# Attention and gated MLP on one core: the row sums of the first 256 queries by matmul, an opening ordered anew

## The chip, the cores and the metric

The kernel runs on one core of a Trainium2 chip. A core has five engines that work beside one another, each with its own queue of instructions that it takes strictly in order: TensorE (PE; its weight loads are listed as PEld), VectorE (DVE), ScalarE (ACT), GpSimd (POOL) and SyncE (SP), which here issues the DMAs. An engine waits for another on semaphores. The metric is the device time in microseconds, from one launch.

## The reference

Eight batches of windowed attention over 8 heads, then a gated MLP on the result:

```python
# q, k, v: (8, 8, 576, 64)
scores = q @ k.T / 8 + slope_h * -(i - j);  masked to 0 <= i - j < 128
attn = exp(scores - max);  attn = attn / (sum(attn) + 1e-9)
x = (attn @ v) as (8, 576, 512)
h = relu(x @ w_in);  u, g = h[:, :, :512], h[:, :, 512:]
g = layer_norm(g);   g = einsum('ts,bsd->btd', w_spatial, g) + b_spatial
out = (u * g) @ w_out
```

w_in and w_out arrive as 64-bit words. They are turned into float32 on the chip, by four or five passes of DVE and ACT over each 128x512 piece (`bits64`).

## The kernel before, in words

Batches 1 to 7 run in a steady pattern: pairs of heads (28 pairs), each with its products (L794), a softmax (L808 to L848), a DMA transpose (L854) and the products with the values (L899), and then, for a whole batch, the units of the MLP: v (L983), u (L1046), s (the spatial product, L1067) and o (L1107).

Batch 0 is different, since nothing is loaded and no weight is converted yet. It works on tiles of 128 queries, named `t` (products, minimum and exponent: `raw_tile`) and `n` (transpose on PE, product with the values: `raw_out`), each digit pair being tile and head pair: `t02` is tile 0 of pair 2. In `raw_tile` PE writes the scores of two blocks into two of four PSUM banks `s`, DVE adds the table and takes the row's extreme (L705), and ACT takes the exponent and, with `accum_out`, the row sum (L709; the accumulator is then read by an instruction of its own). A step `m` (`raw_sums`, L717 and L718) waits for the row sums of all four pairs of a tile and takes the reciprocals. `raw_out` multiplies the probabilities by them (L730 on ACT or L731 on DVE), transposes (L738), copies (L412), multiplies with the values (L753) and copies the result out (L412) to `xt`. The MLP units of batch 0 are the same in float32: v at L976, u at L1038, o at L1099. The first u unit needs all four converted pieces of the u half of w_in; the last pass over such a piece is L449.

What sets the order: the kernel records its steps as a plan, each with an engine (or a choice between ACT and DVE), a weight in ns, a due time and the parts of buffers it reads and writes. A list scheduler (`forward`, `backward`) runs through the plan twelve times and writes the instructions in the order of the best pass. The string OPENING sets the order of recording of the first steps. The weights and due times decide what stands where in each queue; on the chip the queues are then fixed. On PE, 64 matmuls of a tile of ones with itself (`WARM`, L395) are steps of the plan too, and stand wherever the planner saw PE free. A last step adds further matmuls of that kind where the plan has an idle gap on PE (`filler`).

Of the kernel before, what the change touches and what calls it, by code (L numbers as in the profile page):

```python
# [9 lines left out]
F32 = mybir.dt.float32  # L10
# [5 lines left out]
AF = mybir.ActivationFunctionType  # L16
# [39 lines left out]
class Plan:  # L56
# [3 lines left out]

    PASSES, COLD, SLOW = 12, 6000, 9000
    LAG = {"PE": 200, "DVE": 130, "ACT": 130, "POOL": 150, "SP": 2200}

    def __init__(self):
# [42 lines left out]
    def forward(self, due):  # L109

        left = [len(x) for x in self.first]
        at, begun, ended, way = ([0] * len(left) for _ in range(4))
        ready = {e: [] for e in self.LAG}
        free = {**dict.fromkeys(self.LAG, 0), "SP": 700}
        events = [(0, n) for n, k in enumerate(left) if k == 0] + [(700, -1)]
        heapq.heapify(events)
        out, queued, now, dma, lanes = [], dict.fromkeys(self.LAG, 0), 0, 800, []
        while events or any(ready.values()):
            while events and events[0][0] <= now:
                n = heapq.heappop(events)[1]  # L120
                if n >= 0:
                    ways = self.ops[n][0]
                    ends = [max(free[w[0]], now) + queued[w[0]] + w[1] + (700 if w[0] == "DVE" and len(ways) > 1 else 0) for w in ways]
                    k = way[n] = ends.index(min(ends))
                    queued[ways[k][0]] += ways[k][1]
                    heapq.heappush(ready[ways[k][0]], (due[n], n, k))
            for e, heap in ready.items():
                if heap and free[e] <= now:
                    _, n, k = heapq.heappop(heap)
                    weight = self.ops[n][0][k][1]  # L130
                    queued[e] -= weight
                    if e == "SP":
                        dma = max(dma, now)
                        ended[n] = dma = dma + weight * (1.9 if dma < self.SLOW else 1)
                        lanes = [*lanes[-7:], dma + self.LAG[e]]
                        free[e] = max(now + (650 if now < self.SLOW else 500), lanes[0] if len(lanes) == 8 else 0)
                    else:
                        ended[n] = free[e] = now + weight * (2 if e == "PE" and now < self.COLD else 1)
                    begun[n] = now
                    end = ended[n] + self.LAG[e] + self.late.get(n, 0)  # L140
                    out.append(n)
                    heapq.heappush(events, (free[e], -1))
                    for a, whole in self.after[n]:
                        left[a] -= 1
                        at[a] = max(at[a], end if whole else now)
                        if left[a] == 0:
                            heapq.heappush(events, (at[a], a))
            if events:
                now = max(now, events[0][0])
        assert len(out) == len(self.ops)  # L150
        return max(ended), out, way, ended, begun
# [40 lines left out]
                self.filler(int((idle - self.SPARE) * self.FILL / self.filler_ns))  # L192
            self.ops[n][0][best[2][n]][2]()

    SPARE, FILL, UNTIL = 400, 0.5, 95000

    def idle(self, out, way, ended, begun):

        last = None
        for n in out:  # L200
            gap = 0
            if self.ops[n][0][way[n]][0] == "PE":
                if last is not None and self.SLOW < begun[n] < self.UNTIL and begun[n] - ended[last] > self.SPARE:
# [6 lines left out]
def attn_gmlp_kernel(ctx, tc, qk, v, w_in, w_spT, b_sp, w_out, outT):  # L210
# [3 lines left out]
    nc = tc.nc  # L214
# [14 lines left out]
    NB = S // D  # L229

    SWITCH = 190
    SCORES, VALUES, BOTH = 1600, 1800, 2760


    WX = 12
    OPENING = (
# [37 lines left out]
    def act(n, pointers=0):  # L274
        return (45, 188, 284)[pointers] + n / 1.18
# [4 lines left out]
    def pe(*cols):  # L280
        return sum(12 + n / 2.38 for n in cols)
# [1 line left out]
    def pe16(*cols):  # L283
        return sum(2.5 + n / 2.4 for n in cols)

    def dma(n):
        return n / 385


    nhalf = fixed([P, 1], F32, "nhalf")  # L290
# [34 lines left out]
    def xcols(x, a, c0, c1):  # L325
        return parts(x, c0, c1, 32, (a,))
# [220 lines left out]
    def wsp_load(c, due):  # L547
        st = raw_w[c] = plan.buf(work, f"wraw{c}", 1, [P, S], F32)

        def f():  # L550
            nc.sync.dma_start(st(), w_spT[c * P:(c + 1) * P, :])
        plan.add("SP", dma(P * S * 4), due - 4000, f, (), [(st, 0)])

        def f():
            nc.scalar.activation(wsp()[:, c, 1, :].bitcast(BF16), st(), AF.Abs)
        plan.add("ACT", act(S), due, f, [(st, 0)], [(wsp, (c, 1))])
# [75 lines left out]
    def load(b, p, due, pieces, raw=None):  # L632


        raw = raw or plan.buf(work, "qkraw", 3, [P, 2, S], F32)
        src = qk[b, 2 * p:2 * p + 2].rearrange("h d a s -> (h d) a s")
        for t0, t1, d in zip([0] + pieces, pieces, due):
            cs = slice(t0 * P, min(S, t1 * P))
            plan.add("SP", dma(P * 2 * (cs.stop - cs.start) * 4), d, lambda cs=cs: nc.sync.dma_start(raw()[:, :, cs], src[:, :, cs]),
                     (), [(raw, t) for t in range(t0, t1)])  # L640
        return raw

# [2 lines left out]
    def values_load(b, p, due):  # L645
        if b == 0 and p == NP - 1:
            vr = vr3
        else:
            vr = plan.buf(work, *(("vraw", NP) if b % 2 or b == 0 else (f"wraw{p}", 1)), [P, NQ, P], F32)
        vraw[b, p] = vr  # L650
        for t0, t1 in ((0, 2), (2, NQ)) if b == 0 else ((0, NQ),):
            plan.add("SP", dma(P * (t1 - t0) * P * 4), due + 15000 * (t0 > 0), lambda t0=t0, t1=t1: nc.sync.dma_start(vr()[:, t0:t1], v[b, p][:, t0:t1]),
                     (), [(vr, t) for t in range(t0, t1)])

    def values_limit(b, p, due):
# [27 lines left out]
    def raw_tile(p, t, k, raw, due):  # L683
# [15 lines left out]
        for e, i in enumerate(blocks):  # L699
            n = min(i + 1, 3) * D  # L700
            pr = lambda e=e, n=n: slot_ap(k)[:, W - n:W] if e == 0 else slot_ap(k)[:, 512 - n:]
            cols = slot_parts(k, e)

            def f(e=e, n=n, pr=pr):
                nc.vector.tensor_tensor_reduce(pr(), flat(e)[:, :n], tabs()[:, 2 * p + e, W - n:], -0.125, 3e38, ALU.add, ALU.min, st(NM_, e))  # L705
            plan.add("DVE", dve(n), due + 300, f, [(sc[e], 0), (tabs, 2 * p + e)], cols + [key(NM_, e)])

            def f(e=e, pr=pr):
                nc.scalar.activation(pr(), pr(), AF.Exp, bias=st(NM_, e), scale=-1.0, accum_out=st(SM_, e))  # L709
            plan.add("ACT", act(n, 2), due + 600, f, cols + [key(NM_, e)], cols + [key(SM_, e)])  # L710
# [10 lines left out]
    def raw_out(p, t, k, vr, xt, due):  # L721
# [2 lines left out]
        tiles = [x for x in (t - 1, t) if x >= 0]  # L724
        st = lambda e: rstat()[:, t % 2, RC_, e * NP + p:e * NP + p + 1]
        cols = [x for e in range(len(blocks)) for x in slot_parts(k, e)]
        for e, i in enumerate(blocks):
            n = min(i + 1, 3) * D
            pr = lambda e=e, n=n: slot_ap(k)[:, W - n:W] if e == 0 else slot_ap(k)[:, 512 - n:]
            plan.either([("ACT", act(n, 1), lambda e=e, pr=pr: nc.scalar.activation(pr(), pr(), AF.Copy, scale=st(e))),  # L730
# [15 lines left out]
        def f():  # L746
            for j in range(2):
                for n, x in enumerate(tiles):
                    c = n * P + j * D
                    ap = pf(c, c + D)  # L750
                    if len(blocks) == 2:
                        ap = bass.AP(ap.tensor, ap.offset, [ap.ap[0], [len(tiles) * P + D - 2 * j * D, 2], [1, D]])
                    nc.tensor.matmul(xp()[j * D:(j + 1) * D, :m], vr()[:, x, j * D:(j + 1) * D], ap,  # L753
                                     start=(n == 0), stop=(n == len(tiles) - 1), skip_group_check=True)
        plan.add("PE", SWITCH // 2 + 40 + pe(*[4 * m] * len(tiles)), due + 800, f, pcols + [(vr, x) for x in tiles], [(xp, 0)])
        qs = slice(t * P, t * P + m)
        copy(m, lambda: (xt()[:, qs], xp()[:, :m]), due + 1000, [(xp, 0)], xcols(xt, 0, qs.start, qs.stop))

    def clear():
# [380 lines left out]
    def record(kind, b, p):  # L1140
# [124 lines left out]
```

## Time and profile before

| | before |
|---|---|
| time, median of 3 runs | 535.12 us (535.08 to 535.28) |
| profiled execution, its own time | 535.35 us |
| its span, first to last instruction | 533.6 us |
| PE busy | 524.9 us, 98% |
| DVE busy | 441.4 us, 83% |
| ACT busy | 410.3 us, 77% |
| granted TensorE clock, mean | 1.000 |

The profiled execution lies 0.23 us above the median. Its span is 1.75 us shorter than its time. A busy share is an average over the whole span; the stages differ, and the rows below show them one by one. In the rows "128x192" is partitions by elements of one instruction; `idle before` is the time for which the engine did nothing ahead of it. DVE and ACT instructions overlap at their ends by some 0.1 us, so that what one costs its queue is the distance from its start to the next start, not its duration.

### The profile page before, as it was taken

The page shows a single profiled execution, that of the slowest core. Times are in us where ns is not written, and L with a number is a line of the kernel's source. Part 1 is how long each engine was busy: PE and PEld are TensorE (multiplying, and loading weights), DVE is VectorE, ACT ScalarE, POOL GpSimd, SP SyncE. Part 2 cuts the span into 40 slices and gives each one's busy share as a digit, 9 for nine tenths or more (in the row PEclk, how much of TensorE's full clock was granted, in tenths as well). Part 3 has the DMA queues.
Part 4 walks back from the last instruction along what each step waited for, and adds up shares of the span by engine and source line. Part 5 has one row for each costly group of instructions (what it writes and reads, how often), then busy time and mean ns, then how long its engine had stood idle before and what let it go on. Part 6 is the DMA issues. An engine that isn't in the chain of part 4 may idle for free.

```text
span 533.6 us, 15995 instructions
## 1 busy us (share of the span) xinstructions
PE 524.9 (98%) x6118; PEld 380.0 (71%) x6120; DVE 441.4 (83%) x1645; ACT 410.3 (77%) x1289; POOL 29.2 (5%) x75
## 2 busy tenths in 40 slices
PE   9999999999999999999999999999999999999997
PEld 5656567776687668885788758886688758784775
DVE  7999999999997787989999899888998898635440
ACT  7999999979986676969889778777977777634322
POOL 0000020001100010001100010000100010001000
PEclk9999999999999999999999999999999999999999
DMA  7987563987585433699768865765175435410002
GB/s 240 356 304 265 157 113 63 234 182 164 119 173 128 130 74 86 160 213 173 140 143 195 173 140 98 174 157 128 45 142 144 110 68 71 92 47 22 2 1 90
DMA packets 127809, 73.56 MB, mean 138 GB/s; under 512 B 105970, under 2 KB 118386, under 8 KB 127732
## 3 DMA queue, kind: packets, MB, share of 16 engines
q1 hardware_dynamic: 127732, 72.54, 57.7%
q8 instruction: 48, 0.79, 0.6%
q14 instruction: 29, 0.24, 0.1%
HBM read 37.13 MB, written 9.44 MB: 87 GB/s over the span
## 4 chain that ended last, share of the span: by engine, by line
PE 51%; DVE 3%; ACT 1%; issue 0%; DVEq 0%
PE m L1067 13%; PE m L1107 11%; PE m L1046 11%; PE m L983 8%; PE s L794 3%; PE x L899 3%; PE m L1012 1%; DVE pq L848 1%; DVE st L941 0%; DVE prob L808 0%; ACT pq L843 0%; DVE vt L954 0%; DVE vn L994 0%; PE s L899 0%; ACT prob L814 0%; DVE st L946 0%
## 5 line engine op out<-in xcount | busy, mean ns | idle before, releaser
L1067 PE MATMUL m<-wsp,vn 128*128 128x288 f16 x768 | 110.9, 286 | 0.0
L814 ACT ACTIVATE prob<-prob,stat 128x192 f32<-128x192 f32 (+2 forms) x252 | 107.0, 432 | 3.1 <-DVE stat L808 2.8
L843 ACT ACTIVATE pq<-prob,stat 128x192 f16<-128x192 f32 (+2 forms) x252 | 90.2, 429 | 3.9 <-DVE pq L848 1.3
L1067 PEld LDWEIGHTS <-vn 128*128 128x128 f16 x768 | 74.8, 98 | 19.6 <-issue 0.2
L1046 PE MATMUL m<-xt,win 128*128 128x288 f16 x672 | 88.1, 286 | 0.4 <-ACT vt L416 0.4
L848 DVE SCALAR_TENSOR_TENSOR pq<-prob,stat,pq 128x192 f16<-128x192 f32 (+2 forms) x252 | 86.9, 389 | 1.0 <-ACT pq L843 0.8
L1107 PE MATMUL m<-gs,wout 128*128 128x288 f16 x636 | 81.3, 286 | 0.0
L1046 PEld LDWEIGHTS <-win 128*128 128x128 f16 x672 | 65.1, 98 | 19.4 <-issue 1.5
L1107 PEld LDWEIGHTS <-wout 128*128 128x128 f16 x672 | 64.9, 98 | 16.5
L983 PE MATMUL m<-win,xt 128*128 128x512 f16 x336 | 75.5, 379 | 0.2 <-ACT o L1120 0.2
L808 DVE CUSTOM_DVE_ANT_0 prob<-s,tabs 128x192 f32<-128x192 f32 (+2 forms) x252 | 70.3, 329 | 5.9 <-PE s L794 5.7
L983 PEld LDWEIGHTS <-xt 128*128 128x128 f16 x336 | 32.2, 98 | 38.6 <-issue 2.4
L814 ACT ACTIVATION_READ_ACCUMULATOR prob<-prob,stat 128x1 f32 x252 | 49.3, 196 | 0.0
L1083 ACT ACTIVATE gs<-u 128x288 f16<-128x288 f32 x46 | 20.3, 441 | 37.6 <-DVE u L1080 37.2
L794 PE MATMUL s<-qkraw 64*64 64x192 f32 (+1 forms) x1008 | 43.4, 310 | 0.0
L1080 DVE SCALAR_TENSOR_TENSOR u<-m,u 128x288 f32<-128x288 f32 x56 | 25.5, 456 | 21.4 <-PE m L1067 20.5
L899 PEld LDWEIGHTS <-vh 64*64 64x64 f16 x1232 | 34.7, 106 | 9.5 <-issue 8.0
L899 PE MATMUL x<-pt,vh 64*64 64x192 f16 (+2 forms) x1188 | 38.3, 224 | 1.1 <-POOL am L910 1.1
L794 PEld LDWEIGHTS s<-qkraw 64*64 64x64 f32 x1008 | 36.3, 133 | 1.9 <-issue 1.6
L941 DVE BATCH_NORM_STATS2 st<-vt 128x6 f32<-128x512 f32 (+1 forms) x40 | 27.5, 688 | 12.2 <-ACT vt L416 11.8
L950 POOL TENSOR_TENSOR st<-st,nhalf 128x1 f32<-128x1 f32 (+1 forms) x40 | 25.4, 635 | 210.9 <-DVE st L946 179.8
L1087 DVE SCALAR_TENSOR_TENSOR gs<-gs,u 128x288 f16<-128x288 f16 x53 | 24.1, 455 | 10.1 <-ACT gs L1083 9.5
(187 smaller groups left out, 792.1 us busy)
## 6 DMA issues: line engine op xcount, KB each, us to landing
qkraw<-in_qk_dram SPq DMA_DIRECT2D x28, 576.0 KB, 5.0
out_dram<-o SPq DMA_DIRECT2D x63, 144.0 KB, 1.8
vraw<-in_v_dram SPq DMA_DIRECT2D x16, 320.0 KB, 3.7
wraw<-in_v_dram SPq DMA_DIRECT2D x12, 320.0 KB, 3.1
vn<-in_w_in_dram SPq DMA_DIRECT2D x4, 512.0 KB, 7.6
wout<-in_w_in_dram SPq DMA_DIRECT2D x4, 512.0 KB, 7.8
wout<-in_w_out_dram SPq DMA_DIRECT2D x4, 512.0 KB, 4.9
wraw<-in_w_spT_dram SPq DMA_DIRECT2D x4, 288.0 KB, 5.1
```

Source lines behind the costliest of these rows:

```text
L794: nc.tensor.matmul(flat(bank)[rows, c0:c0 + n], raw()[j * D:(j + 1) * D, 0, i * D:(i + 1) * D], raw()[j * D:(j + 1) * D, 1, (i + 1) * D - ...
L808: nc.vector.tensor_tensor_reduce(pt(), flat(bank)[:, c0:c0 + n], tabs()[:, 2 * p + odd, W - n:], -0.125, 3e38, ALU.add, ALU.min, st()[:, N ...
L814: nc.scalar.activation(pt(), pt(), AF.Exp, bias=st()[:, NM, k:k + 1], scale=-1.0, accum_out=st()[:, SM, k:k + 1])
L843: nc.scalar.activation(pq()[:, qc:qc + n], prob()[:, pc:pc + n], AF.Copy, scale=st()[:, RC, k:k + 1])
L848: nc.vector.scalar_tensor_tensor(pq()[:, qc + PLANE:qc + PLANE + n], prob()[:, pc:pc + n], st()[:, RC, k:k + 1], pq()[:, qc:qc + n], ALU.m ...
L899: done.append(nc.tensor.matmul(views[half]()[j * D:(j + 1) * D, x0:x0 + len(ks) * D], l()[rows, kb // 2, j * D:(j + 1) * D], ap, start=(it ...
L941: nc.vector.bn_stats(st()[:m, 0:6], vt()[:m])
L983: nc.tensor.matmul(pt(), xt[c]()[:, a, t * P:(t + 1) * P], w[1, c]()[:, k, :], start=(n == 0), stop=(n == 3 * NC_ - 1))
L1046: nc.tensor.matmul(pt()[:, :HS], w[0, c]()[:, k, d * P:(d + 1) * P], xt[c]()[:, a, hf * HS:(hf + 1) * HS], start=(n == 0), stop=(n == 3 * ...
L1067: nc.tensor.matmul(pt()[:, :HS], l, r, start=(n == 0), stop=(n == len(ops) - 1))
L1080: nc.vector.scalar_tensor_tensor(u(), pt()[:, :HS], GATE * FINE, u(), ALU.mult, ALU.mult)
L1107: nc.tensor.matmul(pt()[:, :HS], wout[d]()[:, w, e * P:(e + 1) * P], gs[d]()[:, a, :], start=(n == 0), stop=(n == 3 * ND - 1))
```

## The change

For the first two tiles of batch 0 (`t < EARLY`, 256 queries) ACT takes the exponent without `accum_out`, no step `m` follows, and the probabilities aren't scaled. Instead PE multiplies the transposed probabilities by a 64-column tile of ones as well, into the upper half of the PSUM bank that takes the product with the values. ACT copies these sums to `sm` and adds 1e-9, DVE takes the reciprocal of `sm` (128x128) and multiplies the product by it on its way to `xt`. The first loads of pairs 1 and 3 are issued by ACT. 13 matmuls of ones stand in the plan in place of 64, and gaps on PE are filled from 3.5 us of the plan on instead of 9. The planner's model of the DMA queue, its early PE weight (COLD) and one PE weight (BOTH) have other values, and the string OPENING is another one.

```diff
-    PASSES, COLD, SLOW = 12, 6000, 9000
+    PASSES, COLD, SLOW = 12, 5000, 9000
...
-                        dma = max(dma, now)
-                        ended[n] = dma = dma + weight * (1.9 if dma < self.SLOW else 1)
-                        lanes = [*lanes[-7:], dma + self.LAG[e]]
+                        dma = max(dma, now) + weight
+                        ended[n] = dma + 0.27 * max(0, dma - now - 600)
+                        lanes = [*lanes[-7:], ended[n] + self.LAG[e]]
...
-    SPARE, FILL, UNTIL = 400, 0.5, 95000
+    SPARE, FILL, FROM, UNTIL = 400, 0.5, 3500, 95000
...
-    SCORES, VALUES, BOTH = 1600, 1800, 2760
+    SCORES, VALUES, BOTH = 1600, 1800, 2660
...
-        "t00 t02 t03 a03 t11 t01 t10 m00 n00 a00 n01 t13 w00 n02 t20 t12 t21 m10 n03 n11 n10 t22 n12 t23 w01 m20 n22 n13 w02 "
+        "t00 D10 a03 t01 t02 n00 n01 X02 t10 n10 w00 t13 t20 t03 n02 n03 t12 t21 n12 n13 t11 n11 t23 t31 t22 w01 m20 n22 n21 "
...
-    def dma(n):
-        return n / 385
+    def dma(n, row=4096):
+        return n / (400 if row > 2560 else 350 if row > 1024 else 240 if row > 512 else 200)
...
-    WARM = 64
+    WARM = 13
+    EARLY = 2
...
+            if b == 0 and t0 == 0 and p % 2:
+                plan.add("ACT", 620, d, lambda cs=cs: nc.scalar.dma_start(raw()[:, :, cs], src[:, :, cs]), (), [(raw, 0)], lag=2200)
+                continue
...
+            if t < EARLY:
+                def f(e=e, pr=pr):
+                    nc.scalar.activation(pr(), pr(), AF.Exp, bias=st(NM_, e), scale=-1.0)
+                plan.add("ACT", act(n, 1), due + 600, f, cols + [key(NM_, e)], cols)
+                continue
...
-        for e, i in enumerate(blocks):
+        for e, i in enumerate(blocks if t >= EARLY else ()):
...
+                    if t < EARLY:
+                        nc.tensor.matmul(xp()[j * D:(j + 1) * D, 2 * P:2 * P + m], ones()[:, :D], ap, start=False, stop=(n == len(tiles) - 1),
+                                         skip_group_check=True)
...
+        if t < EARLY:
+            sm = plan.buf(work, "sm", 2, [P, P], F32)
+            plan.add("ACT", act(m), due + 900, lambda: nc.scalar.activation(sm()[:, :m], xp()[:, 2 * P:2 * P + m], AF.Copy, bias=1e-9), [(xp, 0)], [(sm, 0)])
+            plan.add("DVE", 100 + dve(m), due + 950, lambda: nc.vector.reciprocal(sm()[:, :m], sm()[:, :m]), [(sm, 0)], [(sm, 0)])
+            plan.add("DVE", dve(m), due + 1000, lambda: nc.vector.tensor_tensor(xt()[:, qs], xp()[:, :m], sm()[:, :m], ALU.mult),
+                     [(xp, 0), (sm, 0)], xcols(xt, 0, qs.start, qs.stop))
+            return
...
         elif kind == "m":
-            raw_sums(b, at + 4900)
+            if b >= EARLY:
+                raw_sums(b, at + 4900)
```

How the instructions stand on PE, some ten microseconds into the program, around the first transpose (L738 before, L748 after; `s` are score banks, `x` takes the product with the values, `m` a transpose). Before:

```order
L696 MATMUL s_66<-pt 64x192 x2
L696 MATMUL s_67<-pt 64x192 x2
L395 LDWEIGHTS ones
L395 MATMUL x_70<-ones 128x256
L395 LDWEIGHTS ones
L395 MATMUL x_70<-ones 128x256
L738 MATMUL m<-ident,prob 128x128 x2
L395 LDWEIGHTS ones
L395 MATMUL x_70<-ones 128x256
L696 MATMUL s_68<-qkraw 64x192 x2
```

Now:

```order
L700 MATMUL s_66<-qkraw 64x64 x2
L700 MATMUL s_67<-qkraw 64x128 x2
L748 MATMUL m<-ident,prob 128x128 x2
L700 MATMUL s_68<-qkraw 64x192 x2
L700 MATMUL s_69<-qkraw 64x192 x2
L748 MATMUL m<-ident,prob 128x128 x2
L763 MATMUL x_71<-pq,vraw 64x128
L766 MATMUL x_71<-pq,ones 64x128
L763 MATMUL x_71<-pq,vraw 64x128
L766 MATMUL x_71<-pq,ones 64x128
```

The fill matmuls between the tiles are gone, the first transpose stands after three score tiles instead of seven, and each product with the values is followed by one with the ones.

On DVE, the early part of the softmax of batch 0 (`wx` is a piece of w_in under conversion, ISA the pass over the scores). Before:

```order
L437 TENSOR_SCALAR wx_225<-wx_225 128x512
L441 TENSOR_SCALAR wx_225<-wx_225 128x512
L445 SCALAR_TENSOR_TENSOR wx_225<-vn3_161,wx_225 128x512
L717 TENSOR_SCALAR rstat_102<-rstat_102 128x8
L718 RECIPROCAL rstat_102<-rstat_102 128x8
L449 SCALAR_TENSOR_TENSOR wx_225<-vn3_161,wx_225 128x512
L705 ISA pt_151,rstat_102<-s2_68,tabs_77 128x192
```

Now:

```order
L709 ISA prob_98,rstat_102<-s1_67,tabs_77 128x192
L709 ISA rstat_102 128x1
L774 RECIPROCAL sm_228<-sm_228 128x128
L775 TENSOR_TENSOR xt_250<-x1_71,sm_228 128x128
L709 ISA prob_98,rstat_102<-s2_68,tabs_77 128x192
L709 ISA rstat_102 128x1
L709 ISA prob_98,rstat_102<-s3_69,tabs_77 128x192
L709 ISA rstat_102 128x1
L774 RECIPROCAL sm_243<-sm_243 128x128
L438 TENSOR_SCALAR wx_234<-wx_234 128x512
```

One reciprocal of eight columns per tile has become one of 128 columns per tile and pair, in the queue ahead of further passes over scores and weights.

On DVE again, the end of the conversion of the u half of w_in, ahead of the first u unit (L449 before, L450 after). Before:

```order
L731 TENSOR_SCALAR pt_151<-pt_151,rstat_102 128x192
L449 SCALAR_TENSOR_TENSOR wx_462<-wout2_272,wx_462 128x512
L445 SCALAR_TENSOR_TENSOR wx_399<-wout0_198,wx_399 128x512
L731 TENSOR_SCALAR pt_151<-pt_151,rstat_102 128x192
L449 SCALAR_TENSOR_TENSOR wx_633<-wout3_488,wx_633 128x512
L449 SCALAR_TENSOR_TENSOR wx_399<-wout0_198,wx_399 128x512
```

Now:

```order
L413 COPY pq_99<-m_678 128x256
L413 COPY pq_99<-m_685 128x512
L741 TENSOR_SCALAR pt_129<-pt_129,rstat_102 128x192
L446 SCALAR_TENSOR_TENSOR wx_631<-wout3_503,wx_631 128x512
L741 TENSOR_SCALAR pt_129<-pt_129,rstat_102 128x192
L450 SCALAR_TENSOR_TENSOR wx_631<-wout3_503,wx_631 128x512
```

The last piece is finished as the last of its group in both; two copies of transposes and two scalings, on which late tiles of batch 0 depend, stand just before it now.

## Rows read from the trace of the kernel before

**Rows 1.** Windows by stage: us from start, then busy us per engine, PEclk, DMA.

```profile
0.00:4.80 4.80, 3.81 (x19) 2.70 (x19) 3.81 (x24) 3.30 (x5) 1.02 (x7) 1.00 0.39 100
4.80:10.00 5.20, 5.20 (x68) 3.61 (x67) 2.77 (x23) 3.63 (x17) 0.00 (x0) 1.00 0.94 303
10.00:17.00 7.00, 7.00 (x80) 3.55 (x77) 6.90 (x34) 6.53 (x30) 0.00 (x0) 1.00 1.01 374
17.00:46.00 29.00, 26.60 (x276) 16.82 (x276) 27.77 (x101) 28.75 (x85) 0.00 (x0) 1.00 0.83 284
46.00:140.00 94.00, 92.71 (x942) 62.51 (x942) 91.63 (x344) 89.07 (x278) 6.10 (x13) 1.00 0.74 171
140.00:200.00 60.00, 60.00 (x690) 44.05 (x689) 51.55 (x182) 46.09 (x146) 4.99 (x10) 1.00 0.53 118
```

**Rows 2.** Chain that ended last, in time: start us, us, what.

```profile
260.33 6.19 PE m L1046 x48
...
518.40 11.77 PE m L1107 x96
```

**Rows 3.** Timeline of PE: start us, us, instruction, out<-in, form, count.

```profile
0.99 4.45 PE L395 MATMUL x<-ones 128*128 128x256 bf16 x20 [0.99 <-DVE halves L357]
5.36 0.53 PE L696 MATMUL s<-qkraw 64*64 64x64 f32 x8
...
8.43 1.92 PE L395 MATMUL x<-ones 128*128 128x256 bf16 x16
...
21.01 0.66 PE L753 MATMUL x<-pq,vraw 128*64 128x128 f32 x8
21.60 0.56 PE L696 MATMUL s<-qkraw 64*64 64x192 f32 x8
...
46.67 2.21 PE L1038 MATMUL m<-xt,wx 128*128 128x288 f32 x8
```

**Rows 4.** Lines by form, DVE reciprocals and scalings: count | busy us, mean ns | idle.

```profile
L837 DVE RECIPROCAL stat<-stat 128x5 f32<-128x5 f32 x28 | 5.0, 180 | 0.3
...
L837 DVE RECIPROCAL stat<-stat 128x4 f32<-128x4 f32 x28 | 4.8, 172 | 0.3
...
L718 DVE RECIPROCAL rstat<-rstat 128x8 f32<-128x8 f32 x4 | 0.8, 203 | 0.1
...
L717 DVE TENSOR_SCALAR rstat<-rstat 128x8 f32<-128x8 f32 x4 | 0.7, 170 | 0.0
...
L718 DVE RECIPROCAL rstat<-rstat 128x4 f32<-128x4 f32 x1 | 0.2, 178 | 0.0
L717 DVE TENSOR_SCALAR rstat<-rstat 128x4 f32<-128x4 f32 x1 | 0.2, 170 | 0.6 <-ACT pt L709 0.6
```

**Rows 5.** Timeline of DVE, stage from 16 to 46 us.

```profile
16.73 0.17 DVE L717 TENSOR_SCALAR rstat<-rstat 128x8 f32<-128x8 f32 x1
...
17.05 0.31 DVE L705 CUSTOM_DVE_ANT_0 pt<-s,tabs 128x192 f32<-128x192 f32 x1
...
17.29 0.78 DVE L731 TENSOR_SCALAR pt<-pt,rstat 128x192 f32<-128x192 f32 x3
17.98 0.28 DVE L412 COPY xt<-x 128x128 f32<-128x128 f32 x1
18.18 0.35 DVE L705 CUSTOM_DVE_ANT_0 pt<-s,tabs 128x192 f32<-128x192 f32 x1
...
19.45 0.68 DVE L412 COPY pq<-m 128x512 f32<-128x512 f32 x1
...
43.75 1.28 DVE L449 SCALAR_TENSOR_TENSOR wx<-wout,wx 128x512 int32<-128x512 int32 x2
```

**Rows 6.** Timeline of ACT, one stretch of the opening.

```profile
17.30 0.44 ACT L730 ACTIVATE pt<-pt,rstat 128x192 f32<-128x192 f32 x1
17.65 0.44 ACT L709 ACTIVATE prob<-prob,rstat 128x192 f32<-128x192 f32 x1
...
18.09 0.45 ACT L709 ACTIVATE pt<-pt,rstat 128x192 f32<-128x192 f32 x1
```

More of the change, by code (lines that the diff above doesn't have):

```diff
@@ L202, in idle @@
             if self.ops[n][0][way[n]][0] == "PE":
-                if last is not None and self.SLOW < begun[n] < self.UNTIL and begun[n] - ended[last] > self.SPARE:
+                if last is not None and self.FROM < begun[n] < self.UNTIL and begun[n] - ended[last] > self.SPARE:
                     gap = begun[n] - ended[last]
@@ L551, in f @@
             nc.sync.dma_start(st(), w_spT[c * P:(c + 1) * P, :])
-        plan.add("SP", dma(P * S * 4), due - 4000, f, (), [(st, 0)])
+        plan.add("SP", dma(P * S * 4, S * 4), due - 4000, f, (), [(st, 0)])
         def f():
@@ L638, in load @@
             cs = slice(t0 * P, min(S, t1 * P))
-            plan.add("SP", dma(P * 2 * (cs.stop - cs.start) * 4), d, lambda cs=cs: nc.sync.dma_start(raw()[:, :, cs], src[:, :, cs]),
+            if b == 0 and t0 == 0 and p % 2:
+                plan.add("ACT", 620, d, lambda cs=cs: nc.scalar.dma_start(raw()[:, :, cs], src[:, :, cs]), (), [(raw, 0)], lag=2200)
+                continue
+            plan.add("SP", dma(P * 2 * (cs.stop - cs.start) * 4, (cs.stop - cs.start) * 4), d, lambda cs=cs: nc.sync.dma_start(raw()[:, :, cs], src[:, :, cs]),
                      (), [(raw, t) for t in range(t0, t1)])
@@ L651, in values_load @@
         for t0, t1 in ((0, 2), (2, NQ)) if b == 0 else ((0, NQ),):
-            plan.add("SP", dma(P * (t1 - t0) * P * 4), due + 15000 * (t0 > 0), lambda t0=t0, t1=t1: nc.sync.dma_start(vr()[:, t0:t1], v[b, p][:, t0:t1]),
+            plan.add("SP", dma(P * (t1 - t0) * P * 4, (t1 - t0) * P * 4), due + 15000 * (t0 > 0), lambda t0=t0, t1=t1: nc.sync.dma_start(vr()[:, t0:t1], v[b, p][:, t0:t1]),
                      (), [(vr, t) for t in range(t0, t1)])
@@ L754, in f @@
                                      start=(n == 0), stop=(n == len(tiles) - 1), skip_group_check=True)
-        plan.add("PE", SWITCH // 2 + 40 + pe(*[4 * m] * len(tiles)), due + 800, f, pcols + [(vr, x) for x in tiles], [(xp, 0)])
-        qs = slice(t * P, t * P + m)
+                    if t < EARLY:
+                        nc.tensor.matmul(xp()[j * D:(j + 1) * D, 2 * P:2 * P + m], ones()[:, :D], ap, start=False, stop=(n == len(tiles) - 1),
+                                         skip_group_check=True)
+        plan.add("PE", SWITCH // 2 + 40 + pe(*[4 * m] * len(tiles)) * (2 if t < EARLY else 1), due + 800, f, pcols + [(vr, x) for x in tiles] + [(ones, 0)],
+                 [(xp, 0)])
+        qs = slice(t * P, t * P + m)
+        if t < EARLY:
[5 more added lines that the diff above has]
+            return
         copy(m, lambda: (xt()[:, qs], xp()[:, :m]), due + 1000, [(xp, 0)], xcols(xt, 0, qs.start, qs.stop))
```

14 rows, old and new, of the table OPENING are left out of this document.

## The prediction

> **What bounds the kernel now.** Read the chain of waits first. From 260.33 us on it is one unbroken run of matmuls up to the last units, the final o matmuls from 518.40 included [rows 2]. So the end is a time at which PE is let go, plus PE's own work. The windows by stage say how far back this holds: PE is busy for 60.00 of 60 us between 140 and 200, and for 92.71 of 94 between 46 and 140, so that little more than 1.3 us of waiting is left after 46 us [rows 1]. I therefore take the first u unit of batch 0, which starts on PE at 46.67 [rows 3], as the mark: whatever moves it moves the end, up to that 1.3 us.
>
> What sets the mark is found in the same windows. DVE is busy 6.90 of 7 us from 10 to 17 and 27.77 of 29 from 17 to 46, ACT 28.75 of 29 [rows 1]. Both are full; PE is not short of time there, since its fill matmuls, which compute nothing that is used, stand between 0.99 and 17 us [rows 3]. DVE is idle for long only once, for 5.20 - 2.77 = 2.4 us between 4.8 and 10 us [rows 1], while it waits for the first scores. Its last pass over the w_in pieces that the u unit reads starts as one of two at 43.75 and ends at 45.03 [rows 5], 1.64 us ahead of the mark. So the opening is bound by the DVE and ACT queues, DVE only just behind.
>
> **PE's part.** 51 fill matmuls go. The first 20 stand in a run from 0.99 to 5.36, 0.218 us each; the 16 at 8.43 take 1.92, 0.12 each [rows 3]. That is 7 x 0.218 + 44 x 0.12 = 6.8 us of PE time. 24 float32 products with the ones come in: eight passes, which are four such matmuls of 128 columns, take 21.60 - 21.01 = 0.59 us [rows 3], so 24 take 3.5 us. The seven new fill matmuls, of half the width, take some 0.4. PE has 2.9 us less to do, all of it ahead of the mark, where PE isn't the bound: I count it at nothing. If DVE and ACT were early enough it would count in full, and 2.9 is the most that PE's own part can give.
>
> **ACT's part.** 16 exponents lose the read of the accumulator. An exponent with it takes its queue 18.09 - 17.65 = 0.44 us, and a scaling of the same width, without it, 17.65 - 17.30 = 0.35 [rows 6]: 16 x 0.09 = 1.4 us. Seven scalings fewer are 2.5 us. Eight copies of sums replace copies to xt of the same width. The two DMA issues stand ahead of ACT's first instruction, where it has nothing to compute. ACT gets about 3 us lighter. It still waits for DVE's scores, so this alone moves nothing.
>
> **DVE's part, up to the mark.** Here the sum is made, by counts of instructions in the queue.
> - Seven scalings fewer: three in a row take 17.98 - 17.29 = 0.69 [rows 5], 0.23 each: -1.6.
> - Two steps m fewer, 17.05 - 16.73 = 0.32 each [rows 5]: -0.6.
> - Five copies to xt fewer, 18.18 - 17.98 = 0.20 each [rows 5]: -1.0.
> - One copy of 512 columns and two of 256 fewer: 0.68 less the overlap of 0.08 that the 0.28 copy shows, and half of it each [rows 5]: -1.2.
> - Eight multiplies by the reciprocal, 128 columns out of PSUM: as the copy of that width, 0.20: +1.6. Their second operand could make them dearer, not cheaper; 0.3 is the upper end.
> - One memset of 512 columns comes over from ACT: between the 0.20 and the 0.60 of those copies, +0.4.
> - Conversion passes that changed sides cancel against one reduction that came in; I take 0, with 0.6 either way.
>
> Together -2.4. Then the eight reciprocals of 128 columns, which no row shows. The nearest have 4, 5 and 8 columns: 172 to 178 ns, 180 and 203. A scaling of the same shapes takes 170 ns at 4 and at 8 [rows 4]. So a reciprocal grows with its width as the other does not: (203 - 178) / 4 = 6.3 ns a column by the one line, (203 - 172) / 4 = 7.8 by the other. Carried on by 120 columns that is 0.95 to 1.14 us, less the overlap 0.87 to 1.06 for the queue. The lower end is far away: if width cost no more than in a copy, 0.20. I take 1.0, since every pair of the rows gives a slope and none gives the copy's. Eight cost +8.0, between 1.6 and 8.5.
>
> The Trainium skill (VectorE: DVE Perf Modes, section First, the fixed hardware budget) says that the same pipe runs the reciprocal as an iterative divide with a repeat count of 8. That speaks against this change: at the 0.96 GHz of that page's specifications a column is an estimated 8.3 ns, 128 columns 1.07 us and a fixed part, and the forecast would be about 1 us later than mine. The rows here agree in the slope, 6.3 to 7.8; no row shows the width.
>
> What is won back on DVE is idle time. The first scores can start at 0.99 + 13 x 0.218 = 3.8 us instead of 5.36, so the first wait, some 1 us of the 2.4 before 10 us, goes. I don't count the rest: the first reciprocals stand in the queue behind a transpose, two copies and a product of the same tile, and later passes stand behind them. So 1.0 won, between 0 and 2.4.
>
> DVE's last pass over the u pieces then ends at 45.03 - 2.4 + 8.0 - 1.0 = 49.6 us. Two scalings now stand directly before it; the transpose, copy and product of a late tile follow on PE and ACT before the u unit. I give them 1.0 us (0 to the 1.64 of before): the mark is at 50.6, 3.9 later. Behind the mark PE has a transpose and a product of batch 0 more to do than before, some 0.5 us. Of the 1.3 us of waiting after the mark I let 0.7 go. 3.9 + 0.5 - 0.7 = +3.7 us. The profiled execution's own time is 535.35, which gives 539.05; it lies 0.23 above the median of the runs shown, so I forecast 538.8. With the bounds of the reciprocal at 0.87 and 1.06, and of the idle time, the likeliest case alone spans 537.0 to 540.5.
>
> **The rivals.**
> - *The reciprocal is cheap (faster).* If 128 columns take 0.3 us in the queue, eight cost 2.4, DVE reaches the end of the weights 1.0 us earlier than before, ACT is 3 us lighter, and the mark moves by 1.0 + 0.6 to the left: with +0.5 and no waiting won back, about -1.5 to -2.0, 533.4. The place is the eight L774 rows; it decides from 8R - 2.4 - 1.0 - 0.6 + 0.5 - 0.7 = 0, which is R = 0.53 us. For it: the plan reckons with 0.31. Against it: every slope in [rows 4].
> - *It is dear, but hidden (no change).* The reciprocals stand between passes over w_in pieces that are needed late, and PE, lighter by 2.9 us and with the first products out earlier, could do other tiles meanwhile; also DVE has 60 - 51.55 us to spare between 140 and 200 [rows 1]. Then the time stays near 535.1. Against it: DVE and PE are both full from 46 to 140, so lateness finds no room there.
> - *A slow clock on top (slower still).* The granted clock reads 1.00 throughout [rows 1], but the first 20 fill matmuls take 0.218 each and later ones 0.12 [rows 3], the lower level of 1.2 GHz and the upper of 2.4. Before, PE ran without a break up to there. Now it has 13 fill matmuls and then waits between its first tiles; if it stays at the lower level to 10 us, the first tiles and the products with the ones take twice their time, some 1.5 us more ahead of the first reciprocals: 540.3.
>
> **How the numbers follow.** The forecast has 0.50, the cheap reciprocal 0.20, the hidden one 0.17, the slow clock 0.13. A difference under 0.2%, 1.1 us, can't be told from none. Faster takes the cheap case and a quarter of the hidden one: 0.24. No change is most of the rest of the hidden one: 0.12. Slower is left: 0.64. The range must reach over zero to the cheap case, and up to the slow clock with reciprocals at their dear end: 533.2 to 541.0.
>
> **What would show it.** The rows of L774 in the trace after: near 1.0 us each I am right in the main term, under 0.5 wrong. The last L450 before the first u matmul (L1059) should end near 49.6 and that matmul start near 50.6, with DVE idle for 1 to 2 us between 5 and 10. The spacing of PE's tiles up to 10 us shows the clock. If the reciprocals are dear and the mark is still at or before 46.7, the error is in how DVE bounds the opening; if the mark is late and the end is not, it is in taking PE's work after the mark as fixed.

## The result and the profile after

The changed kernel takes 540.62 us (median of 5 runs, 539.93 to 541.08), the kernel before beside it 535.26 (535.08 to 535.50): a ratio of 1.0099, 95% interval 1.0085 to 1.0113, some 5.3 us slower. The profiled execution took 540.00, 4.65 more than that of before, with a span of 538.2.

First the windows by stage of the changed kernel, in the columns of [rows 1]. Three rows of before follow, cut at its mark (the start of the first u unit of batch 0) and at the point from which its chain of waits is PE alone, then three of after, cut at the new mark 49.36 and at a point that lies as far ahead of the end.

```profile
0.00:4.80 4.80, 3.33 (x21) 2.00 (x21) 3.75 (x24) 2.68 (x4) 1.02 (x7) 1.00 0.45 115
4.80:10.00 5.20, 3.88 (x56) 2.40 (x60) 3.28 (x24) 3.16 (x11) 0.00 (x0) 1.00 0.86 267
10.00:17.00 7.00, 5.96 (x76) 3.91 (x72) 6.36 (x24) 5.67 (x19) 0.00 (x0) 1.00 1.05 393
17.00:46.00 29.00, 26.13 (x258) 17.07 (x257) 28.52 (x103) 26.93 (x82) 0.00 (x0) 1.00 0.78 274
46.00:140.00 94.00, 91.63 (x971) 62.58 (x972) 91.24 (x345) 86.13 (x272) 5.58 (x13) 1.00 0.67 169
```

Before:

```profile
0.00:46.67 46.67, 43.28 (x445) 27.10 (x445) 41.90 (x181) 42.88 (x137) 1.02 (x7) 1.00 0.83 281
46.67:140.00 93.33, 92.04 (x933) 62.08 (x933) 90.96 (x343) 88.40 (x275) 6.10 (x13) 1.00 0.74 170
140.00:260.33 120.33, 119.79 (x1539) 88.78 (x1538) 105.10 (x393) 95.20 (x304) 8.13 (x19) 1.00 0.62 134
```

After:

```profile
0.00:49.36 49.36, 42.07 (x439) 27.27 (x439) 45.27 (x177) 41.72 (x121) 1.02 (x7) 1.00 0.80 276
49.36:140.00 90.64, 88.86 (x939) 60.68 (x940) 87.88 (x337) 82.84 (x266) 5.58 (x13) 1.00 0.66 164
140.00:265.00 125.00, 123.90 (x1547) 91.26 (x1546) 107.54 (x395) 98.45 (x310) 7.97 (x20) 1.00 0.59 137
```

Cut at the end of DVE's last pass over the u pieces instead (45.03 before, 48.42 after, shown below), the first window is:

```profile
0.00:45.03 45.03, 41.64 (x423) 25.93 (x424) 40.26 (x178) 41.24 (x132) 1.02 (x7) 1.00 0.82 281
0.00:48.42 48.42, 41.50 (x430) 26.95 (x430) 44.33 (x175) 40.78 (x119) 1.02 (x7) 1.00 0.80 276
```

The reader is to see two things. DVE is busy for 45.27 us up to the mark instead of 41.90, 3.4 more; it is idle 0.7 less; so the mark is 2.69 later. Up to the last pass it is 44.33 instead of 40.26, 4.1 more. And behind the mark PE's idle time grew: 213.66 - 211.83 = 1.83 us before, 215.64 - 212.76 = 2.88 after, with 0.93 us more work.

The lines that answer to [rows 2], [rows 3], [rows 4] and [rows 5] follow, all of the changed kernel. The reciprocals, by form (count | busy us, mean ns | idle):

```profile
L774 DVE RECIPROCAL sm<-sm 128x128 f32<-128x128 f32 x8 | 7.6, 948 | 0.6 <-ACT sm L773 0.5
L728 DVE RECIPROCAL rstat<-rstat 128x8 f32<-128x8 f32 x2 | 0.4, 204 | 0.1
```

The timeline of DVE, one reciprocal with what starts next, and the last pass over the u pieces:

```profile
18.03 0.95 DVE L774 RECIPROCAL sm<-sm 128x128 f32<-128x128 f32 x1
18.89 0.36 DVE L438 TENSOR_SCALAR wx<-wx 128x512 f32<-128x512 f32 x1
...
47.74 0.68 DVE L450 SCALAR_TENSOR_TENSOR wx<-wout,wx 128x512 int32<-128x512 int32 x1
```

The timeline of PE, its start and the mark:

```profile
0.99 2.95 PE L395 MATMUL x<-ones 128*128 128x256 bf16 x13 [0.99 <-DVE halves L357]
3.87 0.45 PE L700 MATMUL s<-qkraw 64*64 64x64 f32 x8
5.46 0.72 PE L700 MATMUL s<-qkraw 64*64 64x64 f32 x16 [1.14 <-DMA qkraw<-in_qk_dram]
...
49.36 2.21 PE L1059 MATMUL m<-xt,wx 128*128 128x288 f32 x8 [0.37 <-ACT pq L413]
```

The last run of the chain of waits:

```profile
523.03 11.77 PE m L1128 x96
```

A reciprocal of 128 columns takes 0.948 us and 18.89 - 18.03 = 0.86 of the queue; the eight take 6.9. The last pass over the u pieces ends at 48.42, the u unit starts 0.94 later (1.64 before). From the mark to the last run of o matmuls it is 523.03 - 49.36 = 473.67 us; before it was 518.40 - 46.67 = 471.73 [rows 2, 3]. So the change costs 2.69 us ahead of the mark and 1.94 behind it.

### The profile page after: what moved, and what is told of

It is laid out like the page before. It is cut to its first block, busy times and chain, and to the rows that moved or that the text cites. A ratio compares the mean times of both kernels' runs of the same rounds, so it can differ in the third digit from the quotient of the medians.

```text
span 538.2 us, 15998 instructions
## 1 busy us (share of the span) xinstructions
PE 524.4 (97%) x6124; PEld 380.9 (71%) x6124; DVE 443.7 (82%) x1643; ACT 407.5 (76%) x1272; POOL 28.6 (5%) x75
## 4 chain that ended last, share of the span: by engine, by line
PE 78%; DVE 12%; ACT 3%; issue 3%; DMA 2%; SPq 1%; POOL 1%; POOLq 0%; ACTq 0%; DVEq 0%
PE m L1088 20%; PE m L1128 15%; PE m L1067 14%; PE m L1004 11%; PE s L815 6%; PE x L920 5%; PE m L1120 3%; DVE pq L869 2%; PE m L1033 2%; DMA vn<-in_w_in_dram 1%; DVE st L962 1%; DMA qkraw<-in_qk_dram 1%; DVE prob L829 1%; DVE vt L975 1%; DVE sm L774 1%
## 5 line engine op out<-in xcount | busy, mean ns | idle before, releaser
L947 ACT ACTIVATE xt<-x 128x320 f16<-128x320 f32 (+1 forms) x54 | 19.5, 403 | 18.8 <-PE x L920 18.8
```

## The experiments

Five rounds each, against the kernel before on the same chip; the ratio is that to the kernel before. "Mark" is the start of the first u unit of batch 0, "behind" the distance from it to the start of the last run of o matmuls; "scores" is the time that the first eight 64x64 score matmuls take, empty where they stand in a longer group. All three are of the profiled execution.

| kernel | us | ratio (95%) | mark | behind | scores |
|---|---|---|---|---|---|
| before | 535.26 | 1 | 46.67 | 471.73 | 0.53 |
| changed | 540.62 | 1.0099 (1.0085 to 1.0113) | 49.36 | 473.67 | 0.45 |
| e1, cheap reciprocals | 537.61 | 1.0041 (1.0026 to 1.0055) | 47.28 | 473.65 | 0.71 |
| e2, reciprocals twice | 549.75 | 1.0259 (1.0239 to 1.0279) | 59.46 | 473.65 | 0.71 |
| e3, all but the sums | 536.81 | 1.0022 (1.0011 to 1.0033) | 48.19 | 471.73 | 0.71 |
| e4, the sums alone | 542.63 | 1.0131 (1.0114 to 1.0147) | 54.87 | 471.03 | 0.45 |
| e5, changed, again | 540.43 | 1.0098 (1.0085 to 1.0112) | 50.56 | 473.65 | 0.70 |
| e5, 20 fills | 539.54 | 1.0083 (1.0069 to 1.0096) | 49.36 | 473.66 | 0.45 |
| e6, cheap and 20 fills | 536.97 | 1.0036 (1.0023 to 1.0048) | 46.33 | 473.67 | 0.45 |
| e7, true weight | 538.89 | 1.0067 (1.0053 to 1.0081) | 48.92 | 472.17 | 0.70 |
| e8, GpSimd | 683.35 | 1.2767 (1.2750 to 1.2783) | 194.62 | 471.73 | |
| e9, true weight and 20 fills | 537.46 | 1.0039 (1.0027 to 1.0051) | 47.74 | 472.31 | |
| e10, old string, no sums | 539.66 | 1.0078 (1.0063 to 1.0093) | 50.49 | 471.76 | 0.70 |
| e11, sums of 128 queries | 537.32 | 1.0035 (1.0022 to 1.0049) | 48.24 | 472.10 | |

**The price of the reciprocals (e1, e2).** The edits at L774 (of the line that adds the step, only the instruction is shown):

```diff
-lambda: nc.vector.reciprocal(sm()[:, :m], sm()[:, :m])
+lambda: nc.vector.tensor_scalar(sm()[:, :m], sm()[:, :m], 0.0078125, None, ALU.mult)    # e1
+lambda: [nc.vector.reciprocal(sm()[:, :m], sm()[:, :m]) for _ in range(2)]              # e2
```

> The eight 128-column reciprocals (0.95 us each, 0.87 to the next start) become multiplications of the same width by a constant; the plan, its weights and every queue's order stay. Left out: the division by the sums. My theory (the opening is bound by DVE's queue, and the reciprocals are what made it longer): an L774 instruction costs 0.20 to 0.28, DVE gets 8 x 0.65 = 5.2 us lighter, the first u unit comes at 44.5 to 46 instead of 49.36, the time is 535 to 536.5, 4 to 5 us below the changed kernel. Rival (the new order, the loads and the missing fill matmuls cost the time, the reciprocals are hidden): 539 or more.

> Each of the eight reciprocals is done twice in its place, in the same order of every queue. Left out: the division (the second undoes the first). My theory: DVE gets 8 x 0.87 = 7.0 us longer ahead of the mark, nearly all of it is seen at the end: 545.5 to 548. Rival (hidden): below 541.5.

Measured: 537.61 and 549.75. The distance behind the mark is the same to 0.02 us in all kernels of this order (changed, e1, e2, both e5, e6). So the mark does carry the end, one to one, and what lies behind it is the order's own. Both theories of e1 missed in size: the reciprocals aren't hidden (3.0 us come back), yet 2.2 stay.

e2 lies above what I had expected. Its mark came 10.1 later, more than the 7.0 us that I had reckoned. Of that, 1.2 is its start, on which the next experiment is: beside the second run of the changed kernel, which starts alike, the mark is 8.9 later. Of these, 7.7 is DVE's busy time up to the mark (52.99 us against 45.29), since a second reciprocal right behind the first costs the queue 0.99 and not 0.86 (two take 40.74 - 38.89 = 1.85). The other 1.2 is idle time, and 0.78 of it is one wait for PE's scores. The timeline of DVE in e2:

```profile
38.10 0.36 DVE L709 CUSTOM_DVE_ANT_0 pt<-s,tabs 128x192 f32<-128x192 f32 x1 [0.78 <-PE s L700]
...
38.89 1.94 DVE L774 RECIPROCAL sm<-sm 128x128 f32<-128x128 f32 x2
40.74 0.36 DVE L442 TENSOR_SCALAR wx<-wx 128x512 int32<-128x512 int32 x1
```

PE was slow just before that wait. A window of e2 (columns of [rows 1]) and a line of its timeline of PE:

```profile
32.00:37.00 5.00, 4.18 (x23) 3.89 (x24) 4.96 (x12) 1.65 (x4) 0.00 (x0) 0.50 0.02 5
```

```profile
34.12 0.69 PE L766 MATMUL x<-pq,ones 128*64 128x128 f32 x4
```

PE waited for DVE between 20 and 40 us (5.5 us in all), the granted clock then read 0.50, the lower level (1.2 GHz), and a group of four products took 0.69 instead of 0.40 to 0.44. DVE was busy for 4.96 of the 5 us of that window, so the low clock can have cost time only behind it; that the 0.78 is its price is likely and not shown.

**The clock in the opening (e5 twice, e6).** The first 0.71 in the table is not the change of e1: the same eight matmuls had taken 0.45 in the profile of the changed kernel. So I ran the changed kernel again, and with seven more fill matmuls ahead of the scores:

```diff
-        for _ in range(WARM):
-            def f():
+        for k in range(WARM):
+            def f(k=k):
                 x = ones().bitcast(BF16)
-                nc.tensor.matmul(fill()[:, :2 * P], x, bass.AP(x.tensor, x.offset, [x.ap[0], [0, 2], x.ap[1]]), start=True, stop=True)
+                for _ in range(8 if k == 0 else 1):
+                    nc.tensor.matmul(fill()[:, :2 * P], x, bass.AP(x.tensor, x.offset, [x.ap[0], [0, 2], x.ap[1]]), start=True, stop=True)
```

> The changed kernel, unchanged, beside the others on one chip. In its first profile the float32 score matmuls at 3.87 us take 0.45 for eight (upper clock level); with the reciprocals made cheap the same ones took 0.71 (lower level) until 12.3 us. If the level after 13 fill matmuls is left to chance, this run shows 0.45 or 0.71 there and 540 or 541.5; if the chip decides, it shows the lower level and 541 to 542.

> The changed kernel with 20 instead of 13 fill matmuls in the first run of them (seven more in the first step, the order of every queue otherwise the same). Theory that the clock costs time: the scores start at 5.4 and run at the upper level, the first reciprocal stands near 9.6 to 10, time 539.5 to 540.2, 0.5 to 1.5 below the changed kernel on this chip. Rival (the clock is beside the point): as the changed kernel or 0.2 more.

> Cheap reciprocals (multiplications of the same width; the division by the sums is left out) and the 20 fill matmuls together. If the 2.3 us that the cheap reciprocals left over are the clock: 534.5 to 536. If they are the new order behind the mark: 537 to 538.

The timeline of PE in the changed kernel, run again:

```profile
0.99 2.96 PE L395 MATMUL x<-ones 128*128 128x256 bf16 x13 [0.99 <-DVE halves L357]
3.87 0.70 PE L700 MATMUL s<-qkraw 64*64 64x64 f32 x8
...
9.94 0.92 PE L700 MATMUL s<-pt 64*64 64x192 f32 x8
```

With 20 fill matmuls:

```profile
0.99 3.85 PE L396 MATMUL x<-ones 128*128 128x256 bf16 x20 [0.99 <-DVE halves L357]
4.76 0.45 PE L701 MATMUL s<-qkraw 64*64 64x64 f32 x8
...
8.47 0.56 PE L701 MATMUL s<-pt 64*64 64x192 f32 x8 [0.22 <-DMA pt<-in_qk_dram]
```

The same work takes 0.92 or 0.56. I take the longer times for the lower level, since they are near those that stand where the granted clock does read some 0.5 (0.84 to 0.88 for such eight in e10, below); in these openings the column itself reads 1.00. With 13 fill matmuls the first eight score matmuls took 0.70 or 0.71 in six of the seven profiled executions of kernels that have them (the first of the changed kernel is the seventh). With 20 they took 0.45 in e5 and e6; in e9 and e11 they stand in a longer group, and the 64x192 ones behind it took 0.56. The price is the distance between the two marks, 50.56 - 49.36 = 1.20 us, and between the medians 0.89; DVE is busy for the same time up to either mark (45.29 and 45.35), the difference is idle time. Not all of it need be the clock's: the next scores wait for a load of q and k, which let them start at 5.74 in the one and at 5.53 in the other. As to the medians, the spread of the runs (539.82 to 541.17 against 539.39 to 540.00) would fit a kernel that starts now at one level, now at the other, which the runs without a profile don't show.

With the clock out of the way, the cheap reciprocals bring 539.54 - 536.97 = 2.57 us on the same chip, the mark 3.03. By their durations they take 8 x (948 - 224) = 5.8 us off DVE; they overlap with what stands beside them, and DVE's busy time up to the mark, for the same 177 instructions, fell by 4.95 (45.35 to 40.40). It is idle 1.9 us longer. What held it up is seen in the window of 17 to 46 us of e6:

```profile
17.00:46.00 29.00, 26.87 (x289) 18.02 (x281) 27.63 (x103) 28.84 (x86) 0.00 (x0) 1.00 0.88 306
```

ACT is busy 28.84 of 29 us there; in the changed kernel it was 26.93. DVE has 1.4 us to spare. The chain of waits, as the profile infers it, says the same. In the changed kernel, run again, all eight reciprocals stand in it (five of them here; in the first profile it holds four), and it passes to ACT at 41.05, for the last 9.5 us ahead of the mark:

```profile
19.33 0.86 DVE sm L774
21.83 0.87 DVE sm L774
25.29 0.86 DVE sm L774
28.96 0.86 DVE sm L774
31.08 0.86 DVE sm L774
```

In e6 it runs on ACT from 29.04 to the mark at 46.33, but for 1.0 us on DVE; some of its longer pieces:

```profile
32.02 1.14 ACT wsp L557 x2
33.17 1.31 ACT prob L720 x6
35.49 0.68 ACT r L576
41.20 1.05 ACT win L493 x2
42.93 0.77 ACT r L626
```

ACT had become the bound. What is left over after that, 1.9 us above the kernel before, lies behind the mark, as the second theory of e6 had it, whose range it misses by 0.03: its mark is at 46.33, 0.34 ahead of that of before.

**The sums and the rest apart (e3, e4, e10).** e3 sets `EARLY = 0` and moves the steps m of tiles 0 and 1 in the string ahead of the steps n that need them. e4 is the kernel before with the hunks on `EARLY` alone. e10 is `EARLY = 0` with the old string.

```diff
-    EARLY = 2
+    EARLY = 0
...
-        "t00 D10 a03 t01 t02 n00 n01 X02 t10 n10 w00 t13 t20 t03 n02 n03 t12 t21 n12 n13 t11 n11 t23 t31 t22 w01 m20 n22 n21 "
-        "t30 t41 a02 t40 n20 m00 X01 a00 X00 w02 a01 m10 w03 n23 t32 t42 z01 t33 m30 X03 v02 Y00 L10 n30 z02 g00 t43 m40 x03 "
+        "t00 D10 a03 t01 t02 t03 m00 n00 n01 X02 t10 w00 t13 t20 n02 n03 t12 t21 t11 m10 n10 n12 n13 n11 t23 t31 t22 w01 m20 n22 n21 "
+        "t30 t41 a02 t40 n20 X01 a00 X00 w02 a01 w03 n23 t32 t42 z01 t33 m30 X03 v02 Y00 L10 n30 z02 g00 t43 m40 x03 "
```

> The changed kernel without its new sums (EARLY is 0: accum_out, steps m, scaled probabilities for all tiles), with all the rest of the change: loads by ACT, 13 fill matmuls, the planner's model, its string with the steps m of tiles 0 and 1 put in ahead of what needs them. My theory: the sums are what costs, so this stands near the kernel before, 534 to 537. Rival (order and loads cost): 538.5 to 541.

> The kernel before with the new sums alone (old string, old planner's model, all loads by SP, 64 fill matmuls). My theory: DVE's queue gets some 3.4 us longer in the opening as in the changed kernel, without the idle time that was won there: 538.5 to 542. Rival (the sums are nearly free, order and loads cost): 534.5 to 536.5.

> The changed kernel without its new sums (EARLY is 0) and with the string OPENING of before: what is left of the change are the loads by ACT, 13 fill matmuls, and the planner's model and weights. With the new string the same thing took 536.8. If the new string costs the 1.5: 534.5 to 535.5. If the loads, the model or the fewer fill matmuls do: 536.5 to 538.

Without the sums the kernel takes 536.81, 1.5 above the kernel before, with the old distance behind the mark, 471.73 to the hundredth, and its start at the lower level; whether the 1.5 is the price of that start isn't shown, since e3 was not run with 20 fill matmuls. So what the changed kernel loses behind the mark comes with the sums or with the order that the search found for them. It is the order: e4 and e8 have the sums as well, in other orders, and their distances are 471.03 and 471.73. e4 was meant to give the sums' price by itself and doesn't: the planner put 53 fill matmuls ahead of the first scores, which start at 8.59 instead of 5.36, and DVE waits for them:

```profile
8.97 0.23 DVE L706 CUSTOM_DVE_ANT_0 prob<-s,tabs 128x64 f32<-128x64 f32 x1 [4.16 <-PE s L697]
```

e10 is no clean test either, and it missed both of its ranges. PE had no work between 6.2 and 7.6 us, and its clock fell twice, to 0.51 between 9.0 and 11.6 us and to 0.54 between 14.8 and 17:

```profile
9.00:11.60 2.60, 2.60 (x25) 2.44 (x23) 1.66 (x7) 1.81 (x7) 0.00 (x0) 0.51 0.95 311
12.80:14.80 2.00, 1.97 (x18) 1.06 (x18) 2.00 (x10) 1.93 (x9) 0.00 (x0) 1.00 1.05 407
14.80:17.00 2.20, 2.20 (x25) 1.48 (x24) 1.90 (x12) 1.99 (x10) 0.00 (x0) 0.54 1.01 408
```

So the old string under the rest of the change is slower than the new one (539.66 against 536.81, on another chip). That speaks against the new string as what costs the 1.5, but with PE's stop and the two falls of the clock it doesn't show it.

**The weight in the plan (e7, e9).**

```diff
-            plan.add("DVE", 100 + dve(m), due + 950, lambda: nc.vector.reciprocal(sm()[:, :m], sm()[:, :m]), [(sm, 0)], [(sm, 0)])
+            plan.add("DVE", 870, due + 950, lambda: nc.vector.reciprocal(sm()[:, :m], sm()[:, :m]), [(sm, 0)], [(sm, 0)])
```

> The changed kernel with the reciprocal's weight in the plan at 870 ns instead of 308, so that the scheduler knows what it costs; nothing else is edited, the order is searched again. If DVE's work in the opening bounds: 538.5 to 541, since the work is the same wherever it stands. Rival (it is the wrong weight that puts the reciprocals where they block others): 535 to 537.

> The true weight of the reciprocal in the plan (870 ns) and 20 fill matmuls in the first run. If both gains hold beside each other, 538.9 - 1.0 = 537.3 to 538.2, with the mark at 47.5 to 48.5 and 483.6 us from it to the last o unit. Rival (the better order hides the clock): 538.5 to 539.

The same instructions, in the order that the search finds when it knows their cost: 1.5 us less on the chip of the changed kernel's second run (538.89 against 540.43), and 537.46 with 20 fill matmuls, some 2 us above the kernel before. Against the changed kernel with 20 fills, which ran on another chip, the ratio falls from 1.0083 to 1.0039. The mark comes 1.6 earlier (49.36 to 47.74) and 1.35 of the 1.94 us behind it are gone (473.66 to 472.31). e7's time lies at the low edge of the first theory, but that theory held that the work costs the same wherever it stands, and it doesn't: the work costs, and the wrong weight costs about as much again where the clock is out of the way (1.0083 to 1.0039). In e7 and e9 the reciprocals cost DVE as much as ever (0.95 us each), but none of them stands in the chain of waits, which is mostly ACT's there. The 483.6 us that the expectation of e9 names run to a point some 11 us behind that of the table.

**Another engine, and half the sums (e8, e11).** e8 lets GpSimd take the power -1 of `sm` (`neg` holds -1), with 20 fills. e11 is e9 with `EARLY = 1` and the string mended for tile 1.

```diff
-            plan.add("DVE", 100 + dve(m), due + 950, lambda: nc.vector.reciprocal(sm()[:, :m], sm()[:, :m]), [(sm, 0)], [(sm, 0)])
+            plan.add("POOL", 1500, due + 950, lambda: nc.gpsimd.tensor_tensor(sm()[:, :m], sm()[:, :m], neg()[:, 0:1].to_broadcast([P, m]), ALU.pow), [(sm, 0), (nhalf, 0)], [(sm, 0)])    # e8
...
-    EARLY = 2
+    EARLY = 1    # e11
```

> The changed kernel with the reciprocals on GpSimd (sm to the power of -1, 128 columns, the plan reckons 1500 ns), 20 fill matmuls in the first run, the order searched again. No trace so far shows this operation at this width; a power of one column takes 0.62 us there. If DVE's reciprocals are what is left to win, and the power takes under 2 us: the mark (first u unit) at 45 to 47 and 535 to 537.5. If the power takes some 5 us or more, PE waits for the banks that the product holds: 540 or more.

> The new sums for the first 128 queries alone (EARLY is 1, four reciprocals in place of eight), with the true weight (870 ns), the 20 fill matmuls, and the string mended so that the step m of tile 1 stands ahead of what needs it. If the reciprocals' width on DVE is the price, it halves: the mark at 46 to 47.3 instead of 47.74, behind it 483 to 483.7 as in the kernel with no new sums, 534.5 to 536.3, near the kernel before. If the price is the new order whatever the sums: 537 to 538.

Lines by form of GpSimd in e8:

```profile
L777 POOL TENSOR_TENSOR sm<-sm,neg 128x128 f32<-128x128 f32 x8 | 165.6, 20722 | 7.0 <-ACT sm L776 7.0
L974 POOL TENSOR_TENSOR st<-st,nhalf 128x1 f32<-128x1 f32 x32 | 20.5, 640 | 165.0 <-DVE st L970 140.1 <-DVE stat L857 16.9 <-DVE stat L832 4.2
```

20.7 us for 128 columns, 0.64 for one. The opening became a chain of eight powers, the case that the expectation had as 540 or more.

e11 is a miss for my theory: half the reciprocals, and the time over that of the kernel before is that of e9 (1.0035 against 1.0039). In its opening ACT is full (28.93 of 29 us from 17 to 46), and PE waits for ACT's copies and scalings there:

```profile
PE x L764 <- ACT pq L414: 1.6, 4, 0.8
PE m L749 <- ACT pt L741: 1.1, 2, 0.8
```

With the true weight the width of the reciprocals is no longer what bounds the opening, as far as these two orders show. No version here beats the kernel before.

## Why the prediction was right, and where its working was not

The forecast of 538.8 had the direction, and 540.62 lies within its range; the likeliest case alone, 537.0 to 540.5, ends just under it. (By the bounds that it names, 0.87 to 1.06 for a reciprocal and 0 to 2.4 of idle time, that case would span 536.4 to 540.3.) Step by step:

- *PE's chain from the mark to the end*: right, and more exactly than I had put it. Six executions of one order, with marks from 46.33 to 59.46, have the same distance to within 0.02 us.
- *The reciprocals*: 0.86 in the queue against 1.0 taken, just under the lower end of 0.87 to 1.06. The slope is (948 - 204) / 120 = 6.2 ns a column, that of the lower pair of [rows 4]. The estimate of 8.3 ns that I worked out from the Trainium skill's repeat count (VectorE: DVE Perf Modes, First, the fixed hardware budget) is a third too high here; the measurement decides. That width counts at all is what both said.
- *DVE's sum*, up to the last pass over the u pieces: +4.1 us of busy time against -2.4 + 8.0 = +5.6. Of that, 1.1 is the size of the reciprocal, and the rest got lighter by 2.8 instead of 2.4. Idle time won was 0.7 against 1.0. The pass ended at 48.42, not 49.6, and from there to the mark it was 0.94 where I had 1.0: the mark stood at 49.36, not 50.6.
- *ACT's part*: the terms, 1.4 and 2.5, make 3.9 and not 3. Up to the mark ACT's busy time fell by 1.2 (42.88 to 41.72); other pieces stand ahead of the mark there now, among them five conversions of 3.0 us (L492). I had both queues as bounds and gave ACT no part of its own in the forecast; e6 shows that it was the next bound.
- *What failed: "Of the 1.3 us of waiting after the mark I let 0.7 go", with the +0.5 of PE work.* I put -0.2 behind the mark; it was +1.94. The 1.3 was short as well: it ends at 200 us, and up to 260.33 the kernel before waits for 1.83. The waits of PE between the mark and 265 us are:

```profile
PE x L920 <- POOL am L931: 1.1, 4, 0.3
PE m L1004 <- ACT vt L417: 1.1, 2, 0.7
PE m L1088 <- DVE gs L1096: 0.7, 1, 0.7
```

The first of them was there before as well; the other two, the v units' wait for ACT's copies and the s unit's for DVE's g, are new but for 0.2. Of these two it is the one for g that goes with the distance: e3, with the distance of before, has 0.9 of the wait for the copies and none for g, nor have e7 and e9 any for g, which got 1.35 to 1.5 of the 1.94 back. Added to that is the moved work, a product of 64 columns and a transpose of late tiles, 53.43 - 52.68 = 0.75 us where I had 0.5; in the timeline of PE after the mark:

```profile
52.68 0.46 PE L763 MATMUL x<-pq,vraw 128*64 128x64 f32 x8
53.06 0.44 PE L748 MATMUL m<-ident,pt 128*128 128x128 f32 x2
53.43 1.53 PE L815 MATMUL s<-qkraw 64*64 64x192 f32 x36
```

Less waiting after a later mark was an assumption; a new order brings its own waits. The two errors, 1.2 too much ahead of the mark and 2.1 too little behind it, partly cancelled: that 540.62 is as near to 538.8 as it is, is in part luck.

- *The cheap reciprocal, rival*: its condition (under 0.53 us) wasn't met, and e6 shows that it would not have made the kernel faster: 536.97 with 0.22 us, where I had worked out 533.4. That sum was also at odds with itself: -1.6 + 0.5 with no waiting won back is -1.1, 534.0, and only with the 0.7 does it give -1.8. It took DVE's saving as the mark's, where ACT takes over with the mark at 46.33, and it left out the 1.94 behind the mark.
- *The hidden one*: fell with e1 and e2.
- *The slow clock on top*: not in the first profile (0.45), but in the second run of the same kernel (0.70): at most 1.2 us at the mark where I had 1.5. It was no case beside the forecast, but part of it in some executions.

What makes up the 5.3 us, as far as the runs carry it (on the chip of e5 and e6): 0.9 the start (the clock, and perhaps the load), 2.6 the width of the reciprocals as they stand in this order, and 1.9 left over, for which the distance behind the mark (+1.94) is enough. It isn't a sum of independent parts: a true weight in the plan brings back 1.35 of the last as well.

Open: why the search, with the true weight or with four reciprocals, still ends 2 us above the kernel before. Their marks are 1.1 and 1.6 us later than that of before, their distances 0.6 and 0.4 longer. ACT is full in the opening of e6, e9 and e11 and carries the chain of waits there, but it was nearly as full before (28.75 of 29), and no run took work off it.

## What to carry to other kernels

Where one engine carries the end, mark the point at which it is let go and measure the distance from there to the end: it stays put while the order does, and splits a difference in two. An operation that moves between engines or changes its width needs its own measured weight in a planner; here 308 ns in place of 870 cost some 1.5 to 2.4 us beyond the work itself. And taking work off a full engine pays only up to the next full one: 5.0 us off DVE gave 3.

## What the runs showed of the hardware

- PE's pace at the start isn't settled by 13 fill matmuls (2.95 us of work from 0.99 us on). The same kernel ran eight 64x192 float32 score matmuls in 0.56 in one execution and in 0.92 until about 12 us in another. With 20 (3.6 to 4.5 us) they took 0.56. The granted clock read 1.00 through both openings; if this is the clock, its level shows in the durations alone there. Where the column did fall, to 0.54 between 14.8 and 17 us of e10, the same eight took 0.84 to 0.88.
- A reciprocal on DVE takes 204 ns for 8 columns and 948 for 128, which is 6.2 ns for each column between; a multiplication of 128 columns by a constant takes 224. One costs the queue 0.86 us, a second right behind it on the same tile 0.99 (e2).
- GpSimd's power takes 20.7 us for 128 columns, against 0.64 for one.
